# Weights held until the filters' last group, and three small operations moved off VectorE's product chain, in a fused FFT filter and swish MLP kernel

## The chip, the cores and the metric

The kernel runs on one core of one Trainium2 chip. The metric is device time in microseconds (us). A profile of one execution comes with each kernel; its times are also in us, counted from the first instruction. In its lines PE is TensorE's matmuls, PEld its weight loads, DVE is VectorE, ACT is ScalarE, POOL is GpSimd and SPq is the queue in which SyncE issues DMAs. L446 is line 446 of that kernel's source; lines after the change's added line are one higher in the changed kernel.

Runs marked slow are left out: one of the first runs of the kernel before took 1008.37 us. "Rounds" are executions of the kernels compared, taken together; e1 to e7 ran on one chip, e9 to e16 on another, each group with the kernel before beside it. Ratios are the mean time of one kernel's fast runs over that of the other's fast runs of the same rounds, so they are not quite the ratios of the medians that are quoted.

## The reference, cut to what matters

```python
def _attn_ref(x, filt_r, filt_i):          # x: 8 x 3008 x 256
    X = np.fft.rfft(x, axis=1)
    Y = X * (filt_r + 1j * filt_i)[None]   # filters: 1505 x 256
    return np.fft.irfft(Y, n=x.shape[1], axis=1).astype(np.float32)

def _moe_ref(x, w_in, w_out, beta):        # 24064 tokens, 256 -> 2048 -> 256
    h = x @ w_in
    g = h * (1.0 / (1.0 + np.exp(-beta * h)))
    return (g @ w_out).astype(np.float32)
```

The FFT along the sequence is done as matmuls: 3008 = 47 x 64, first a stage over 47, then one over 64 with the filter in between, then both back. `g` is computed as silu(beta * h), and 1/beta is folded into `w_out`.

## The kernel before

Two stretches matter. The **setup** (0 to 38 us) does all of batch 0's FFT. The **main loop** is 752 steps (47 blocks of 512 tokens, 16 feature blocks each): a step is two matmuls `hps`, one SiLU on ScalarE (`gT`) and four matmuls `acc`. Between the steps, the FFT stages of the next batches are woven in.

In the setup, GpSimd waits for a part of the filters (`held`), and only then issues the loads of the weights and of batch 1's input:

```python
# N1 = 47, M = 64, H = 32, NK = 24, KG = 6, J = 32, JG = 8, P = 128
FG = ((0, KG), (KG, KG), (2 * KG, 2 * KG))   # filter groups: first rows and number
# group 0 is issued by GpSimd; groups 1 and 2 by SyncE:
for h in (1, 0):      # group 1: high halves first, then low halves
    ...
for h in (0, 1):      # group 2: low halves first, then high halves
    ...
held = setup.tile([P, 1], F32, name="held", tag="held")
for p0 in (H, M + H):                        # high halves of group 1
    gp.tensor_copy(held[p0 : p0 + H], fri[p0 : p0 + H, 2 * KG - 1, :1])
load_win(0); load_win(1); load_wout(0)       # cut: one per line in the kernel
xs[1] = load_x(1, X_HALVES[:2])              # batch 1, first half
# later, at i == 3: load_wout(1), load_x(1, X_HALVES[2:], xs[1]), load_wout(2), load_wout(3)
```

Twelve pairs of products with the filters then run on VectorE. Around them stand the table copies and beta:

```python
for i in range(NK // 2 + FLAG):
    if 0 < i < NK // 2:
        product(i)           # two VectorE tensor_tensor, pb_t and qb_t, out of PSUM
    ...
    if i in TAB:             # (1, 2, 5, 6, 8, 9): turn a table on PE, copy it from PSUM
        n = TAB.index(i)
        table3(1 + n // 2, 2 - 2 * (n % 2), n % 2 == 0)()   # True: ScalarE copies
    if i == 3:
        ...
        mark3 = dpool.tile([1, D], BF16, name="mark3", tag="mark3")
        nc.sync.dma_start(mark3[:], xs[1][:1, J - 1, :])    # the "marker"
        ...
        nc.tensor.transpose(bps[:], bt[:], id_f[:])
        nc.vector.tensor_copy(beta_sb[:], bps[:])
        nc.vector.reciprocal(rbeta_sb[:], beta_sb[:])
    if i == 9:
        table4()
    if i >= FLAG:
        inverse3(i - FLAG)
...
for at in (0, M):                            # first third of the repeated filters
    for go in load_filter(frr, filt_r, at, 0, JG, nc.sync):
        go()                                 # four loads, 256 KB each, on SyncE
```

Of the kernel before, what the change touches and what calls it, by code (L numbers as in the profile page):

```python
# [11 lines left out]
ACT = mybir.ActivationFunctionType  # L12
# [12 lines left out]
M = 64  # L25
H = M // 2
NK = 24
J = 32
KG = 6
# [8 lines left out]
def kernel(  # L38
# [10 lines left out]
    nc = tc.nc  # L49
# [37 lines left out]
    fri = consts.tile([P, NK, D], F32, name="fri", tag="fri")  # L87
# [10 lines left out]
    beta_sb = consts.tile([P, NFB], F32, name="beta_sb", tag="beta_sb")  # L98
# [6 lines left out]
    def evac(dst, src, on_act, scale=None):  # L105
        if on_act:
            nc.scalar.activation(dst, src, ACT.Copy, scale=1.0 if scale is None else scale)  # L107
        elif scale is None:
            nc.vector.tensor_copy(dst, src)  # L109
        else:  # L110
            nc.vector.tensor_scalar_mul(dst, src, scale)  # L111

    def load_x(b, parts, t=None):
        if t is None:
            t = xpool.tile([NP, J, D], BF16, name="xg", tag="xg")
        xv = x[b].rearrange("(p j) d -> p j d", j=J)
        for p0, p1, j0, j1 in parts:
            nc.gpsimd.dma_start(t[p0:p1, j0:j1, :], xv[p0:p1, j0:j1, :])  # L118
        return t
# [20 lines left out]
    def staged(i):  # L140
        return frr[:, NK - NFB + i * WG : NK - NFB + (i + 1) * WG, :]

    def load_wout(i):
        nc.gpsimd.dma_start(
            staged(i),
            moe_w_out[i * WG * P : (i + 1) * WG * P, :].rearrange("(fb fp) j -> fp fb j", fp=P),
        )
# [52 lines left out]
    gp = nc.gpsimd  # L200
# [75 lines left out]
    def t2_part(h, part):  # L276
        u, r = us[h], rs[h]
        ks_ = slice(h * NH, (h + 1) * NH)
        if part == 0:
            nc.scalar.activation(t2[:, ks_, 2, :], u[:], ACT.Sin, scale=TWO_PI)  # L280
        elif part == 1:
            nc.scalar.activation(r[:], u[:], ACT.Abs)
        else:
            for cols, sgn, b in ((slice(0, H), -1.0, hp), (slice(H, M), 1.0, hm)):
                nc.scalar.activation(
                    t2[:, ks_, 1, cols], r[:, :, cols], ACT.Sin, scale=sgn * TWO_PI, bias=b[:]
                )

    def t2_more(h, eng):
        ks_ = slice(h * NH, (h + 1) * NH)  # L290
        nc.vector.tensor_scalar_mul(t2[:, ks_, 4, :], t2[:, ks_, 1, :], -1.0)
        eng.tensor_copy(t2[:, ks_, 3, :], t2[:, ks_, 2, :])
        eng.tensor_copy(t2[:, ks_, 0, :], t2[:, ks_, 1, :])
# [56 lines left out]
    def table3(i, part, on_act, own=None):  # L350
        pt = own or opsum.tile([P, KG, P], BF16, name="pt", tag="acc")
        for e in range(KG):
            nc.tensor.transpose(
                pt[:, e, :],
                t2[:, KG * i + e, part : part + 2, :].rearrange("p c k -> p (c k)"),
                ident[:],
            )
        dst = t3 if part else t3b

        def go():  # L360
            if i > 0:
                evac(dst[:, KG * i : KG * i + KG, :], pt[:], on_act)
                return
            if part:
                evac(dst[:, 0, :], pt[:, 0, :], on_act, 0.5)
            else:
                nc.vector.tensor_scalar_mul(dst[:, 0, :], pt[:, 0, :], keep[:])
            evac(dst[:, 1:KG, :], pt[:, 1:KG, :], on_act)

        return go  # L370
# [21 lines left out]
    def turn_a(i, on_act):  # L392
        if i % 2 == 0:
            a2s.append(a2pool.tile([P, KG, D], BF16, name="a2", tag="a2"))
        pb = opsum.tile([P, 3, D], BF16, name="pb", tag="acc")
        for e in range(3):
            k1 = 3 * i + e
            for dc in range(NDC):
                nc.tensor.transpose(
                    pb[:, e, dc * P : (dc + 1) * P],  # L400
                    a_t[:, dc, k1, :, :].rearrange("p j a -> p (j a)"),
                    ident[:],
                )
        evac(a2s[-1][:, 3 * (i % 2) : 3 * (i % 2) + 3, :], pb[:], on_act)


    held = setup.tile([P, 1], F32, name="held", tag="held")
    for p0 in (H, M + H):
        gp.tensor_copy(held[p0 : p0 + H], fri[p0 : p0 + H, 2 * KG - 1, :1])
    def load_win(h):  # L410
        fs = slice(h * FF // 2, (h + 1) * FF // 2)
        gp.dma_start(win_sb[:, :, fs], moe_w_in[:, fs].rearrange("(dc p) f -> p dc f", p=P))
# [13 lines left out]
    def product(i):  # L426
        g, kk = divmod(2 * i, KG)
        p_t = pqpool.tile([P, 2, D], BF16, name="pb_t", tag="p_t")
        q_t = pqpool.tile([P, 2, D], BF16, name="qb_t", tag="q_t")
        pss = []  # L430
        for part in (3, 1):
            if part == 3:
                ps = fpsum.tile([P, 2, D], F32, name="ps2", tag="f")
            else:
                ps = hpsum.tile([P, 2, D], F32, name="ps2q", tag="hps")
            for e in range(2):
                nc.tensor.matmul(
                    ps[:, e, :],
                    lhsT=t2[:, 2 * i + e, part : part + 2, :].rearrange("p c k -> p (c k)"),
                    rhs=a2s[g][:, kk + e, :],  # L440
                    start=True,
                    stop=True,
                )
            pss.append(ps)
        for dst, ps in zip((p_t, q_t), pss):
            nc.vector.tensor_tensor(dst[:], ps[:], fri[:, 2 * i : 2 * i + 2, :], ALU.mult)  # L446
        pq[i] = (p_t, q_t)
# [34 lines left out]
    def table4():  # L482
        for src, dst in ((t1b, t4b), (t1, t4)):
            tp = opsum.tile([KP, NP], BF16, name="tp", tag="acc")
            nc.tensor.transpose(tp[:], src[:], ident[:NP, :NP])
            nc.scalar.activation(dst[:], tp[:], ACT.Copy)
# [4 lines left out]
    for i in range(NK // 2 + FLAG):  # L491
        if 0 < i < NK // 2:
            product(i)
        if i % 3 < 2 and i // 3 < 3:
            turn_a(2 + 2 * (i // 3) + i % 3, True)
        if i < 3:
            t2_part(1, i)
        if i in TAB:
            n = TAB.index(i)
            table3(1 + n // 2, 2 - 2 * (n % 2), n % 2 == 0)()  # L500
        if i == 3:
            t2_more(1, nc.vector)
            load_wout(1)
            if B > 1:
                load_x(1, X_HALVES[2:], xs[1])
                mark3 = dpool.tile([1, D], BF16, name="mark3", tag="mark3")
                nc.sync.dma_start(mark3[:], xs[1][:1, J - 1, :])
            load_wout(2)
            load_wout(3)

            bps = hpsum.tile([P, NFB], F32, name="bps", tag="hps")
            nc.tensor.transpose(bps[:], bt[:], id_f[:])
            nc.vector.tensor_copy(beta_sb[:], bps[:])
            nc.vector.reciprocal(rbeta_sb[:], beta_sb[:])
        if i == 9:
            table4()
        if i >= FLAG:
            inverse3(i - FLAG)

# [292 lines left out]
    for s in range(len(steps) + LAG):  # L812
        if s < len(steps):
            i, fb = steps[s]
# [26 lines left out]
        if s >= LAG:  # L841
            i, fb = steps[s - LAG]
# [64 lines left out]
```

## Time and profile before

| | |
|---|---|
| time, first three runs | 792.77 and 792.15 us, and a slow one of 1008.37 |
| profiled run | span 788.4 us |
| PE busy | 777.5 us, 99% |
| first SiLU of the main loop | 38.90 us |

The page's first lines and its chain of waits (shares of the span):

```profile
span 788.4 us, 15540 instructions
PE 777.5 (99%) x6111; PEld 547.9 (69%) x6111; DVE 394.4 (50%) x647; ACT 597.4 (76%) x920; POOL 144.6 (18%) x143
PE 90%; DMA 5%; DVE 3%; issue 1%; POOL 0%; DVEq 0%; ACT 0%; POOLq 0%; SPq 0%; ACTq 0%
```

PE sets the time from the loop's start to its end. A change in the setup can gain only by starting the loop earlier. The timeline of VectorE (start, duration, engine, line, operation, out<-in, shape; in brackets the idle time before) around product 6 and around the last t3b copy:

```profile
25.69 0.68 DVE L446 TENSOR_TENSOR qb_t<-ps2q,fri 128x512 bf16<-128x512 f32 x1
27.01 0.69 DVE L446 TENSOR_TENSOR pb_t<-ps,fri 128x512 bf16<-128x512 f32 x1 [0.64 <-PE ps L437]
27.62 0.68 DVE L446 TENSOR_TENSOR qb_t<-ps2q,fri 128x512 bf16<-128x512 f32 x1
...
31.67 0.68 DVE L446 TENSOR_TENSOR qb_t<-ps2q,fri 128x512 bf16<-128x512 f32 x1
32.27 0.54 DVE L109 COPY t3b<-pt 128x768 bf16<-128x768 bf16 x1
32.73 0.68 DVE L446 TENSOR_TENSOR pb_t<-ps,fri 128x512 bf16<-128x512 f32 x1
```

After product 6 VectorE has no gap until the last product, so whatever ends its wait there sets the loop's start. The bracket names PE, but PE's matmuls for product 6 were over by 25.7 us. This is the case of a wait for several semaphores of which the profile names the wrong one. The trace's raw rows have a semaphore wait of VectorE from 24.23 to 26.87 us, on the semaphores of filter group 2. It really waited for a DMA. And the t3b copy costs 0.46 us of the chain (32.27 to 32.73).

### The profile page before, as it was taken

What the parts mean: (1) busy time and instruction counts of PE and PEld (TensorE: products, weight loads), DVE (VectorE), ACT (ScalarE), POOL (GpSimd) and SP (SyncE); (2) the same over time, 40 slices, a digit from 0 to 9 for tenths busy, and PEclk for the clock granted to TensorE, in tenths of its full rate; (3) what the DMA queues carried; (4) which work ended last, traced back from release to release, by engine and by line L of the source; (5) the groups of instructions that cost most, each with busy time, mean ns of one, the idle gap of its engine ahead of it and who ended that gap; (6) DMA issues with size and microseconds to landing.
All of it is one profiled execution on the core that took longest, in us unless ns stands there. A gap on an engine that the chain in (4) does not pass through costs nothing.

```text
span 788.4 us, 15540 instructions
## 1 busy us (share of the span) xinstructions
PE 777.5 (99%) x6111; PEld 547.9 (69%) x6111; DVE 394.4 (50%) x647; ACT 597.4 (76%) x920; POOL 144.6 (18%) x143
## 2 busy tenths in 40 slices
PE   8899999999999999999999999999999999999997
PEld 5766667766777667876668766686667766776665
DVE  7847835646536564465635746267462761500101
ACT  6887886886678866788677876778767788677776
POOL 9422500420014200131002310024000340000000
PEclk9999999999999999999999999999999999999999
DMA  9978687116901187012860238412370214100101
GB/s 193 233 199 214 161 207 206 48 67 187 234 27 67 48 214 206 28 67 94 198 176 27 95 103 186 151 55 85 103 215 29 74 67 127 51 31 28 54 27 54
DMA packets 84057, 91.46 MB, mean 116 GB/s; under 512 B 4434, under 2 KB 74212, under 8 KB 82962
## 3 DMA queue, kind: packets, MB, share of 16 engines
q1 hardware_dynamic: 80880, 73.95, 30.6%
q0 software_dynamic: 2816, 16.26, 10.6%
q8 instruction: 48, 0.79, 0.4%
q10 hardware_dynamic: 288, 0.26, 0.1%
q14 instruction: 25, 0.20, 0.1%
HBM read 57.16 MB, written 46.66 MB: 132 GB/s over the span
## 4 chain that ended last, share of the span: by engine, by line
PE 90%; DMA 5%; DVE 3%; issue 1%; POOL 0%; DVEq 0%; ACT 0%; POOLq 0%; SPq 0%; ACTq 0%
PE acc L860 40%; PE hps L825 39%; PE ps L621 3%; PE ps L546 2%; PE ps L643 2%; PE ps L669 2%; DMA fri<-in_filt_i_dram 1%; DMA d<-a 1%; DVE ost L109 1%; DMA xg<-in_x_dram 1%; DMA mark<-xg 1%; DMA a<-d 0%; DVE qb_t L446 0%; DVE q_t L658 0%; DVE pb_t L446 0%
## 5 line engine op out<-in xcount | busy, mean ns | idle before, releaser
L834 ACT ACTIVATE gT<-hps,beta_sb 128x512 bf16<-128x512 f32 x752 | 516.8, 687 | 175.2 <-PE hps L825 165.5
L860 PE MATMUL acc<-wout_sb,gT 128*128 128x256 bf16 x3008 | 455.1, 272 | 1.2 <-ACT ost L107 0.2
L825 PE MATMUL hps<-y,win_sb 128*128 128x512 bf16 (+8 forms) x1730 | 447.7, 351 | 0.0
L860 PEld LDWEIGHTS <-gT 128*128 128x128 bf16 x3008 | 285.4, 98 | 132.4 <-issue 4.3
L825 PEld LDWEIGHTS <-win_sb 128*128 128x128 bf16 x1730 | 164.9, 98 | 24.3 <-issue 0.2
L659 POOL TENSOR_TENSOR v_t<-p_t,q_t 128x512 bf16<-128x512 f32 x84 | 106.7, 1271 | 374.5 <-DVE q_t L658 371.6
L109 DVE COPY ost<-acc 128x512 f32<-128x512 f32 (+1 forms) x88 | 56.2, 677 | 193.6 <-PE acc L860 190.6
L109 DVE CAST a<-ps 96x512 bf16<-96x512 f32 x96 | 65.8, 686 | 86.1 <-PE ps L621 83.7
L111 DVE TENSOR_SCALAR y<-ps 128x376 bf16<-128x376 f32 (+1 forms) x119 | 64.4, 545 | 63.1 <-PE ps L546 62.9
L654 DVE TENSOR_TENSOR p_t<-ps,frr 128x512 f32<-128x512 f32 x84 | 58.1, 692 | 32.4 <-PE ps L643 29.8
L658 DVE TENSOR_TENSOR q_t<-ps,fri 64x512 f32<-64x512 f32 x84 | 58.3, 694 | 1.2
L655 DVE SCALAR_TENSOR_TENSOR q_t<-ps,fri 64x512 f32<-64x512 f32 x84 | 57.5, 684 | 1.1
L546 PEld LDWEIGHTS <-zz 96*128 96x128 bf16 x512 | 35.3, 97 | 28.9
L107 ACT ACTIVATE z<-ps 128x512 bf16<-128x512 f32 x84 | 49.5, 590 | 0.8 <-PE ps L669 0.7
L621 PE MATMUL ps<-xg,t 94*96 94x512 bf16 x112 | 41.9, 381 | 0.0
L546 PE MATMUL ps<-t,zz 96*128 96x94 bf16 x448 | 36.7, 204 | 0.0
L118 POOL DMA_DIRECT2D xg<-in_x_dram x22 | 12.1, 557 | 114.3 <-PE acc L860 97.7
L669 PE MATMUL ps<-v_t,t 128*128 128x256 bf16 x168 | 32.1, 273 | 0.6 <-DVE q_t L658 0.6
L643 PE MATMUL ps<-a,t 128*128 128x256 bf16 x168 | 32.1, 273 | 0.3 <-DMA a<-d 0.3
L643 PEld LDWEIGHTS <-t 128*128 128x128 bf16 x168 | 15.9, 98 | 15.0 <-issue 0.4
L621 PEld LDWEIGHTS <-t 94*96 94x96 bf16 x112 | 13.8, 123 | 12.1
L669 PEld LDWEIGHTS <-t 128*128 128x128 bf16 x168 | 15.4, 98 | 8.4 <-DVE q_t L658 1.4
(119 smaller groups left out, 195.8 us busy)
## 6 DMA issues: line engine op xcount, KB each, us to landing
out_dram<-ost SPq DMA_DIRECT2D x80, 256.0 KB, 2.1
d<-a SPq DMA_DIRECT2D x28, 384.0 KB, 3.7
a<-d SPq DMA_DIRECT2D x28, 384.0 KB, 5.1
d<-z SPq DMA_DIRECT2D x28, 384.0 KB, 2.3
zz<-d SPq DMA_DIRECT2D x28, 384.0 KB, 6.6
xg<-in_x_dram POOLq DMA_DIRECT2D x6, 1280.0 KB, 10.1
frr<-in_filt_r_dram SPq DMA_DIRECT2D x12, 256.0 KB, 7.5
out_dram<-ost SPq DMA_DIRECT2D x18, 128.0 KB, 3.6
```

What stands on the lines that cost most here:

```text
L109: nc.vector.tensor_copy(dst, src)
L111: nc.vector.tensor_scalar_mul(dst, src, scale)
L546: nc.tensor.matmul(ps[:, e, :NP], lhsT=zz[:, jj + e, dc * P : (dc + 1) * P], rhs=tab[:], start=True, stop=True,)
L621: nc.tensor.matmul(ps[:KP], lhsT=t1[:], rhs=s["x"][:, 2 * i : 2 * i + 2, :], start=True, stop=True)
L643: nc.tensor.matmul(ps[:, e, :], lhsT=t2[:, k0 + e, 3:5, :].rearrange("p c k -> p (c k)"), rhs=s["a2"][g][:, kk + e, :], start=True, stop=True,
L654: nc.vector.tensor_tensor(p_t[:], ps[:], frr[:, ks_, :], ALU.mult)
L658: nc.vector.tensor_tensor(q_t[:M], ps[M:P], fri[M:P, ks_, :], ALU.mult)
L659: nc.gpsimd.tensor_tensor(v_t[:], p_t[:], q_t[:], ALU.add)
L669: nc.tensor.matmul(ps[:, e, :], lhsT=t3[:, k0 + e, :], rhs=v_t[:, e, :], start=True, stop=True)
L825: nc.tensor.matmul(hps[:, pos - t0 : pos - t0 + ln], lhsT=win_sb[:, dc, fb * P : (fb + 1) * P], rhs=ys[b][:, dc, n0 : n0 + ln], start=(dc ...
L834: nc.scalar.activation(gT[:, :tn], hps[:, :tn], ACT.Silu, scale=beta_sb[:, fb : fb + 1])
L860: nc.tensor.matmul(acc[tb // per][:, tb % per, :], lhsT=gT[:, tb * P : (tb + 1) * P], rhs=wout_sb[:, fb, :], start=(fb == 0 and tb % per = ...
```

## The change

The intent is to give the DMA engines to the filters alone until the last group is (nearly) there, and to take from VectorE what isn't a product while the products run.

```diff
-    for p0 in (H, M + H):
-        gp.tensor_copy(held[p0 : p0 + H], fri[p0 : p0 + H, 2 * KG - 1, :1])
+    for p0 in (0, M):
+        gp.tensor_copy(held[p0 : p0 + H], fri[p0 : p0 + H, NK - 1, :1])
@@ the loop over the products
-            table3(1 + n // 2, 2 - 2 * (n % 2), n % 2 == 0)()
+            table3(1 + n // 2, 2 - 2 * (n % 2), n % 2 == 0 or n == 5)()
@@
+        if i == 11:
+            table4()
 
             bps = hpsum.tile([P, NFB], F32, name="bps", tag="hps")
             nc.tensor.transpose(bps[:], bt[:], id_f[:])
-            nc.vector.tensor_copy(beta_sb[:], bps[:])
+            nc.scalar.activation(beta_sb[:], bps[:], ACT.Copy)
+        if i == NK // 2:
             nc.vector.reciprocal(rbeta_sb[:], beta_sb[:])
-        if i == 9:
-            table4()
```

The gate moves from the high halves of group 1 to the low halves of group 2. (Group 2's high halves, the very last, aren't waited for.) Below, "the gate" is the first part and "the relief" the rest. Beta's transpose and table4 move to the end of the products.

## The prediction

> **What bounds the kernel.** On the profile page TensorE matmuls are busy 777.5 of 788.4 us (99%), and the chain of waits is 90% PE. Everything that the change touches lies in the first 38 us: the first step of the main loop (matmul hps) starts at 38.26 us. From about 17 to 35 us the chain runs through VectorE: the timeline shows 12 pairs of filter products (pb_t, qb_t), 0.68 us each and one every 0.60 us, with few gaps. After 38 us PE is close to saturated, so the change can only shift the loop's start; nothing in the loop itself changes.
>
> **What changes.**
> 1. VectorE loses beta's copy and reciprocal before product 4 (timeline: 23.59 to 23.95, 0.36 us) and the last t3b copy (32.27 to 32.73, 0.46 us). ScalarE takes the t3b copy (its 128x768 copies take 0.81 us, issue about 0.7 us apart) and beta's copy. For that one the Trainium skill, "ScalarE: Activation LUTs", What ACT_TABLE_LOAD costs, gives 186 ns + 0.833 ns per element, so an estimate of 0.2 us; the similarly small t4b copy took 0.24 here. ScalarE is busy 3.08 us of the 5 from 30 to 35 us (windows view), so this fits. The reciprocal (0.25 us) falls into VectorE's 0.36 us hole before z_t. Beta's transpose no longer takes an hps buffer before product 4, for which PE waited 0.37 us at 22.57; late, it holds inverse 9 back until qb_t 10 is done, but inverses 9 and 10 (0.44 us each) fit behind product 11.
> 2. The gate (held) moves from the high halves of filter group 1 to the low halves of group 2. The semaphore landings of those are at about 21.3 and 22.7 us, so GpSimd's weight issue moves from 18.72 to about 23.1 us. Weight packets, however, first moved at about 23.3 us: they stood behind the filters' packets. The Trainium skill, "DMA: Bandwidth & Descriptors", Queues, rings and completion order, says that each engine round-robins between queues; here it looks nearly first come, first served, with mixing only at the tail. So the weights really move by only 0.5 to 1.5 us.
> 3. VectorE's product 6 waited for the last filter transfer: a semaphore wait from 24.23 to 26.87 us, released when its last two DMA engines landed (26.44, 26.83; the other 14 had by 25.4), of which 0.64 us was idle. In those two engines the last ten packets mixed with weights. With weights issued at 23.1 and moving from about 24.3, part of the mixing stays, since the gate is the low half and the high halves land last. I expect landing at about 26.3.
>
> **Sum.** 0.46 us is sure (t3b). The 0.36 us of beta and the 0.64 us of waiting are worth what the landing gains: at most 1.0, expected 0.4. Total 0.9 us, at most 1.5, on the loop's start. Later weights cost nothing: win lands about 28 to 31 (needed 38.3), wout's quarters are scaled four or more us before use, x's first half of batch 1 lands at 36 (needed 39.1). scale_wout(0) moves from 33.0 to about 34.2, needed 40.7.
>
> Predicted: 791.9 us, range 790.4 to 793.4; faster by over 2%: 0.01, within 2%: 0.97, slower: 0.02.
>
> **What would show it.** First hps matmul at about 37.4 instead of 38.26; no t3b copy on VectorE at 32; product pairs 9, 10, 11 without a gap; win's issue at about 23.1; weights landing up to 1.5 us later; the idle before product 6 smaller or gone; nothing different after 45 us but the shift.
>
> **What would make it wrong.** Weights or batch 1's x landing so late that PE waits in the first block; beta's late transpose stalling PE at the products' end; the loop absorbing the shift; run-to-run noise (792.15 to 792.77) larger than the effect, or slow runs such as the one of 1008.

## More of the kernel before

The marker makes SyncE wait until batch 1's second half has landed (it reads a row of the load that brings 80 of its 94 partitions; in the profile before that load landed at 41.08 us and the marker was issued at 41.10). Everything that SyncE issues later stands behind it, in program order: first the four `frr` loads, then the four stores of batch 1's first stage:

```python
apool = pool("apool", 3)                     # three buffers for a1
def s1(b, i, on_act):
    g, jj = divmod(2 * i, JG)
    if jj == 0:
        s["a1"] = apool.tile([KP, JG, D], BF16, name="a1", tag="a1")
    ...                                      # one matmul, ps1
    evac(s["a1"][:, jj : jj + 2, :], ps[:KP], on_act)
    if jj + 2 == JG:
        nc.sync.dma_start(s["d1r"][:, g * JG : (g + 1) * JG, :], s["a1"][:])
```

Batch 1 needs four a1 tiles and there are three buffers, one of them used by batch 0's `zz` at first. So the fourth tile takes the buffer of the first, and may be written only when the first store has landed.

SyncE's queue (its last line here is the first a1 store), and then VectorE's first a1 copy after its wait for that store:

```profile
41.10 0.24 SPq L507 DMA_DIRECT2D mark<-xg  x1
41.38 0.32 SPq L131 DMA_DIRECT2D frr<-in_filt_r_dram  x1
...
43.23 0.39 SPq L626 DMA_DIRECT2D d<-a  x1
```

```profile
50.66 1.31 DVE L109 CAST a<-ps 96x512 bf16<-96x512 f32 x2 [2.33 <-DMA d<-a]
```

VectorE waits 2.33 us for the first store. PE doesn't: from 50 to 56 us it is busy for 6.00 of 6.00 us (the windows view; shown with the result). It still had matmuls to do.

## The result

The changed kernel took 793.41 us (median of 6 runs, 792.48 to 795.84), against 792.15 us (median of the five fast runs) for the kernel before on the same chips. The ratio is 1.0027, with a 95% interval from 1.0006 to 1.0047. So it is within 2%, but slower where 0.9 us of gain was forecast, and 0.01 us above the range.

The page after, and the timelines that answer to those above:

```profile
span 791.7 us, 15448 instructions
PE 771.6 (97%) x6015; PEld 547.6 (69%) x6111; DVE 394.1 (50%) x645; ACT 597.4 (75%) x922; POOL 144.5 (18%) x143
PE 90%; DVE 4%; DMA 3%; issue 2%; ACT 1%; DVEq 0%; ACTq 0%; SPq 0%
```

(Some 96 matmul records are missing from this trace, so PE's busy time isn't compared.)

```profile
26.05 0.69 DVE L446 TENSOR_TENSOR pb_t<-ps,fri 128x512 bf16<-128x512 f32 x1 [1.15 <-DMA fri<-in_filt_i_dram]
...
31.90 0.68 DVE L446 TENSOR_TENSOR qb_t<-ps2q,fri 128x512 bf16<-128x512 f32 x1
32.50 0.68 DVE L446 TENSOR_TENSOR pb_t<-ps,fri 128x512 bf16<-128x512 f32 x1
```

The setup did what was hoped. Product 6 starts 0.96 us earlier, there is no t3b copy at 32 us, and the first SiLU comes at 37.48 instead of 38.90: 1.42 us earlier. Then SyncE's queue, and VectorE's a1 copy:

```profile
43.33 0.24 SPq L507 DMA_DIRECT2D mark<-xg  x1
43.61 0.32 SPq L131 DMA_DIRECT2D frr<-in_filt_r_dram  x1
...
45.47 9.68 SPq L627 DMA_DIRECT2D d<-a  x4
```

```profile
52.74 1.28 DVE L109 CAST a<-ps 96x512 bf16<-96x512 f32 x2 [5.67 <-DMA d<-a]
```

Everything on SyncE is 2.2 us later than in the profile before. VectorE waits 5.67 us for the first store, and now PE waits with it. First, three lines of the changed kernel's list of waits from 46 to 56 us (engine, line, what it waited for: us, times, longest; the list of the kernel before has no wait of PE there). Then PE's busy time from 50 to 56 us, of the kernel before and of the changed one:

```profile
DVE a L109 <- DMA d<-a: 5.7, 1, 5.7
PEld L547 <- issue: 2.9, 1, 2.9
PE ps L547 <- DVE a L109: 2.6, 1, 2.6
```

```profile
50.00:56.00 6.00, 6.00 (x48) 4.02 (x46) 1.67 (x3) 5.47 (x11) 0.00 (x0) 1.00 0.49 138
```

```profile
50.00:56.00 6.00, 3.33 (x26) 2.22 (x26) 1.64 (x3) 3.26 (x7) 0.00 (x0) 1.00 0.72 210
```

The second column of these two is the stretch's length, the third PE's busy time; the third number from the end is the clock that TensorE was granted, as a share of full speed. And the chain of waits of the changed kernel runs, in this stretch, through the store alone:

```profile
45.47 7.16 DMA d<-a
...
52.74 0.70 DVE a L109
...
53.48 0.33 PE ps L547 x4
```

A ledger is useful here. The 752 SiLUs are the same in all kernels, so the start of SiLU number n in one profile minus its start in the first profile of before tells where time was lost. In the changed kernel the difference is -1.42 us at step 0 and -1.26 at step 10. (The 0.16 us go at step 3: batch 1's first half landed at 37.87 us, and PE's first matmul with it could start only at 37.91.) It is +1.52 from step 13 to step 83, +3.31 from step 84, and stays there to the end (+3.34). Two places lose: steps 11 to 13 lose 2.77 us, and step 84 loses 1.79. For the first, the lines give the sum: VectorE's copy is 2.08 us later (50.66 to 52.74) and the loop came 1.26 us earlier to the place. The rest, 2.08 + 1.26 - 2.77 = 0.57 us, is the slack that the kernel before had. The same sum with this slack is tried on three other profiles below the table.

### The profile page after: what moved, and what is told of

Same layout as the page of the kernel before. It is cut to its first block, busy times and chain, and to the rows that moved or that the text cites. A ratio compares the mean times of both kernels' runs of the same rounds, so it can differ in the third digit from the quotient of the medians.

```text
span 791.7 us, 15448 instructions
## 1 busy us (share of the span) xinstructions
PE 771.6 (97%) x6015; PEld 547.6 (69%) x6111; DVE 394.1 (50%) x645; ACT 597.4 (75%) x922; POOL 144.5 (18%) x143
## 4 chain that ended last, share of the span: by engine, by line
PE 90%; DVE 4%; DMA 3%; issue 2%; ACT 1%; DVEq 0%; ACTq 0%; SPq 0%
PE acc L861 41%; PE hps L826 37%; PE ps L622 3%; PE ps L547 3%; PE ps L644 2%; DMA d<-a 2%; PE ps L670 2%; DVE ost L109 1%; DMA a<-d 1%; DVE q_t L659 0%; DVE a_t L109 0%; DVE qb_t L446 0%; DVE q_t L656 0%; ACT a L107 0%; PE pw L187 0%
## 5 line engine op out<-in xcount | busy, mean ns | idle before, releaser
L826 PE MATMUL hps<-y,win_sb 128*128 128x512 bf16 (+8 forms) x1636 | 427.4, 350 | 0.1
```

Of the source, the lines that this page charges most:

```text
L826: nc.tensor.matmul(hps[:, pos - t0 : pos - t0 + ln], lhsT=win_sb[:, dc, fb * P : (fb + 1) * P], rhs=ys[b][:, dc, n0 : n0 + ln], start=(dc ...
```

## The experiments

**Theory A.** The gate makes batch 1's input land later, the marker holds SyncE until then, and the first store, behind the marker and 1 MB of `frr` loads, lands too late for the recycling of the a1 buffers. **Theory B** puts the loss on the work moved to ScalarE and VectorE. Later rivals are named with the runs.

The table has the profile of every run. Columns: the start of product 6 (when the filters' last group is there); the first SiLU; when the first a1 store had landed, from the trace's raw semaphore rows; the us lost against the first profile of before at steps 11 to 16, between step 16 and step 83, and at steps 84 to 88; and the measured ratio to before.

| run | product 6 | first SiLU | store landed | 11-16 | 16-83 | 84-88 | ratio (95%) |
|---|---|---|---|---|---|---|---|
| before | 27.01 | 38.90 | 50.5 | 0 | 0 | 0 | 1 |
| after | 26.05 | 37.48 | 52.6 | +2.77 | 0 | +1.79 | 1.0027 (1.0006 to 1.0047) |
| e1_gate_only | 26.08 | 37.97 | 52.6 | +4.02 | 0 | -0.42 | 1.0030 (1.0014 to 1.0047) |
| e2_relief_only | 27.55 | 38.98 | 52.8 | +1.57 | 0 | -0.42 | 1.0006 (0.9991 to 1.0021) |
| e3_after_frr_late | 26.88 | 38.31 | 48.0 | 0 | +3.62 | +0.54 | 1.0019 (1.0001 to 1.0037) |
| e7_relief_frr_late | 27.21 | 38.65 | 46.1 | 0 | +3.27 | +3.28 | 1.0050 (1.0029 to 1.0071) |
| e9_after_frr_mid | 26.23 | 37.66 | 47.0 | 0 | 0 | +0.74 | 0.9968 (0.9944 to 0.9992) |
| e10_after_frr_mid_nomark | 25.96 | 37.39 | 47.3 | 0 | 0 | +1.00 | 0.9974 (0.9950 to 0.9999) |
| e11_before_frr_mid_nomark | 27.39 | 39.28 | 46.9 | 0 | 0 | -0.36 | 0.9990 (0.9966 to 1.0013) |
| e12_relief_frr_mid_nomark | 27.59 | 39.02 | 47.6 | 0 | 0 | -0.42 | 0.9992 (0.9968 to 1.0017) |
| e13_after_again | 26.18 | 37.61 | 52.4 | +3.68 | 0 | +0.74 | 0.9998 (0.9969 to 1.0026) |
| e14_before_again | 28.27 | 40.17 | 51.4 | 0 | 0 | -0.42 | 0.9981 (0.9953 to 1.0010) |
| e15_frr_mid_beta_early | 26.30 | 37.73 | 47.9 | 0 | 0 | +0.81 | 0.9967 (0.9941 to 0.9993) |
| e16_frr_mid_t3b_vector | 25.78 | 37.68 | 47.7 | 0 | 0 | -0.42 | 0.9953 (0.9922 to 0.9984) |

**What the table doesn't show: the clock.** The traces also record the clock that TensorE was granted. In four of these profiles it stood, within the loop, at half of full speed for 3.41 us, from the end of a stall or up to 1.1 us after it: in e1 from 53.46 us, in e13 from 53.50, in e3 from 72.61, and in e7 twice, from 72.33 and from 137.19. From e13, the windows view of that stretch, and matmuls of its chain of waits before and in it:

```profile
53.50:56.90 3.40, 3.40 (x15) 1.82 (x12) 0.62 (x2) 1.74 (x4) 0.00 (x0) 0.50 0.50 140
```

```profile
42.98 0.44 PE acc L861 x4
43.42 0.45 PE hps L826 x2
...
53.90 0.85 PE acc L861 x4
54.75 0.85 PE hps L826 x2
```

PE is busy all the time there, at half the rate. Half of 3.41 us, about 1.7 us, is an estimate of what each such stretch costs. With it, the sum from the lines closes for the three other profiles that stalled at step 11. The lateness of the a1 copy, plus the lead that the loop had at step 10, minus the slack of 0.57 us, gives 1.56 us for e2 (1.57 measured). It gives 2.37 for e1 and 2.01 for e13, and with the 1.7 added 4.1 and 3.7 (4.02 and 3.68 measured). The changed kernel's first profile had no such stretch, though PE stood idle for 2.62 us in it, and for only 2.22 in e1 and 1.85 in e13; what decides it isn't shown here.

The time of the changed kernel thus depends on chance too. Every run lists its mean granted clock: 0.999 or 1.000 in the profiles without such a stretch, 0.997 or 0.998 in those with one, 0.994 with two. The six runs of e1 have 0.995 to 0.998; the six first runs of the changed kernel 0.996 to 0.999; e9's six 0.999 to 1.000.

### The gate alone

The kernel before with only the first hunk of the diff:

```diff
-    for p0 in (H, M + H):
-        gp.tensor_copy(held[p0 : p0 + H], fri[p0 : p0 + H, 2 * KG - 1, :1])
+    for p0 in (0, M):
+        gp.tensor_copy(held[p0 : p0 + H], fri[p0 : p0 + H, NK - 1, :1])
```

> The kernel before with only the gate moved (weights wait for the low halves of filter group 2); VectorE and ScalarE as before. Theory A (the gate makes batch 1's input land 2 us later, SyncE stands in order behind its marker, so the first stage's stores come late and the recycling of the a1 buffers stalls PE at step 11): first SiLU (gT) about 0.6 us earlier than before's 38.90, because the filters land earlier; the first store of a lands at about 52.6 us as in the changed kernel, and from step 13 on the loop is 1.3 to 1.7 us behind before, whatever the start gained. Time 793 to 795 us, ratio 1.001 to 1.004. Theory B (the loss comes from the moved work on ScalarE and VectorE): ratio 0.999 to 1.000 and no stall at step 11.

Measured: 793.4 us (median of 6), ratio 1.003. The first SiLU is 0.93 us early (0.6 was expected), the store lands at 52.6, and steps 11 to 16 lose 4.02 us. The net delay after step 13 was then 3.1 us, twice the 1.3 to 1.7 expected, so the stall's size was missed and its place was right: about 1.7 us of it is the half clock, which the expectation didn't count. With VectorE's and ScalarE's work as before, the gate alone brings the stall and a loss like that of the change; theory B falls.

### The relief alone

The changed kernel with the old gate:

```diff
-    for p0 in (0, M):
-        gp.tensor_copy(held[p0 : p0 + H], fri[p0 : p0 + H, NK - 1, :1])
+    for p0 in (H, M + H):
+        gp.tensor_copy(held[p0 : p0 + H], fri[p0 : p0 + H, 2 * KG - 1, :1])
```

> The changed kernel with the old gate. Theory A: the last filter transfer lands as before (about 26.8 us), so only the t3b copy's 0.46 us is gained: first SiLU 0.4 to 0.6 us earlier, no stall at step 11 (the first store of a lands at about 50.5 us), loop 0.4 to 0.6 us ahead to the end; ratio 0.9985 to 1.000. Theory B: step 11 or the stage before it is late, ratio above 1.001.

Measured: 791.57 us, ratio 1.0006, not to be told from 1. In its profile the filters landed half a microsecond later than in the first profile of before, and so the first SiLU came no earlier. The expectation of no stall at step 11 was wrong for this execution. The marker was released at 43.50 us, since one of batch 1's DMA shares came late, and 1.57 us was lost. So the old gate doesn't exclude this stall; in the kernel before it was near. It also shows what the marker does while the `frr` loads are in front: in the six profiles with this order, with either gate, the first store landed 8.7 to 9.4 us after the marker was issued (before 41.10 and 50.5, e2 43.50 and 52.8).

### The repeated filters moved out of the way, too far

The changed kernel (e3), and with the old gate (e7), with the first four `frr` loads behind the reads of the second stage:

```diff
-    for at in (0, M):
-        for go in load_filter(frr, filt_r, at, 0, JG, nc.sync):
-            go()
@@ uf(), issued after a2_read(1)
-            for k0 in range(JG, NK, JG)
+            for k0 in range(0, NK, JG)
```

> The changed kernel with the first four loads of the repeated filters (frr) moved on SyncE from before the stores of a to behind the second-stage reads. Theory A: the first store no longer queues behind 1 MB of filters; it is issued at about 43.6 us and lands by 48 instead of 52.6, no wait of VectorE for it and no PE stall at step 11; loop about 1.4 us ahead of before until step 80. Ratio 0.997 to 0.999, unless the later stall at step 84 (1.8 us in the changed kernel's profile) stays; with it 0.999 to 1.001. Rival (the stall is set by the late input alone): the stall at step 11 stays over 1.5 us and the ratio is 1.001 to 1.004.

> Old gate, relieved VectorE, and the frr loads moved behind the second-stage reads as in e3. Theory A: start 0.4 to 0.6 us earlier than before, VectorE's 2.3 us wait for the first store gone, ratio 0.998 to 1.000; e3 is better by up to 1 us since it has the filters' earlier landing too. Rival: the gate costs by contention alone, then this one beats e3 by over 1 us.

Measured: e3 792.82 us, ratio 1.0019; e7 794.24 us, ratio 1.0050. The stall at step 11 is gone in both, as theory A has it. But the loads now come late for their own use, at step 30. VectorE's line in e3:

```profile
69.35 0.69 DVE L651 TENSOR_TENSOR p_t<-ps,frr 128x512 f32<-128x512 f32 x1 [5.02 <-DMA frr<-in_filt_r_dram]
```

The time didn't improve, so the expected times of both were wrong, for a cost that I hadn't counted. In both profiles about 1.7 us of the loss between steps 16 and 83 is the half clock after that wait. Still, the place of the loads decides which wait there is.

### The repeated filters after the second store

The changed kernel with the four loads between the second and the third store (e9):

```diff
@@ s1(), after the store of a1
         if jj + 2 == JG:
             nc.sync.dma_start(s["d1r"][:, g * JG : (g + 1) * JG, :], s["a1"][:])
+            if b == 1 and g == 1:
+                for at in (0, M):
+                    for go in load_filter(frr, filt_r, at, 0, JG, nc.sync):
+                        go()
@@ after the loop over the products
-    for at in (0, M):
-        for go in load_filter(frr, filt_r, at, 0, JG, nc.sync):
-            go()
```

> The changed kernel; the first four frr loads are issued by SyncE after the second store of a instead of before the first one; the marker stays. e3 showed that without them in front there is no stall at step 11, and that behind the second-stage reads they are late themselves (4 us at steps 30 to 32). Here both should be gone: first store issued at 43.5 to 44.2, landed by 48.5; frr landed by about 52, used from 66; start 0.6 to 1.4 us ahead of before's profile and no stall over 0.5 us at steps 11 to 13 and 30 to 32. Ratio 0.997 to 1.000 if the order on SyncE was the whole loss; the rival (the later input and weights cost PE time by themselves) says 1.001 to 1.003.

Measured: 788.68 us (788.2 to 790.98), ratio 0.9968, interval 0.9944 to 0.9992. No stall at steps 11 to 13 nor at 30 to 32. SyncE's queue and the windows view of e9:

```profile
42.62 0.24 SPq L507 DMA_DIRECT2D mark<-xg  x1
42.97 2.21 SPq L623 DMA_DIRECT2D d<-a  x2
45.23 0.53 SPq L131 DMA_DIRECT2D frr<-in_filt_r_dram  x1
```

```profile
50.00:56.00 6.00, 6.00 (x54) 4.32 (x52) 1.42 (x3) 5.59 (x10) 0.00 (x0) 1.00 0.82 201
```

Issue to landing of the first store falls from 7.2 us in the changed kernel to 4.0 here (the view of the store's DMAs; 7.3 in the first profile of before). Of the gain of the start, 1.24 us in this profile, 1.02 us are kept from step 3 to step 83. (The rest goes where PE waits for batch 1's first half.) This version is faster than before in the same rounds. Its slowest run, 790.98 us, is also below the changed kernel's fastest of all its runs, 791.58, but that comparison is across different rounds.

### With and without the marker, and on the other kernels

The marker's two lines are taken out as well, for the changed kernel (e10), the kernel before (e11) and the relief alone (e12):

```diff
-                mark3 = dpool.tile([1, D], BF16, name="mark3", tag="mark3")
-                nc.sync.dma_start(mark3[:], xs[1][:1, J - 1, :])
```

> As e9, also without the marker copy that holds SyncE until batch 1's input has landed. The first store is issued when its data are there (about 41.8 us). If the marker was what made the store late, it lands 1 to 2 us earlier than in e9; if the weights ahead in the DMA rings are what it waits for, it lands when it did in e9 (47 to 48.5 us). Time as e9 within 1 us either way, ratio 0.997 to 1.000.

> The kernel before with the same two edits as e10. If the kernel before often loses a part at step 11 too (its profile is one of its fastest runs and shows 2.3 us of VectorE's wait for the first store hidden in slack), ratio 0.997 to 0.9995; if it does not, 0.9995 to 1.001.

> e10 with the old gate. Theory: the gate's own worth is the earlier landing of the last filter group, 0.5 to 1 us, so e10 is better than this one by that much; t3b's 0.46 us makes this one better than e11. Ratio 0.9975 to 1.000. Rival: the gate is worth nothing or less even with the order on SyncE mended; then this one is level with e10 or better.

Measured: e10 789.6 us, ratio 0.9974; e11 790.93, 0.9990; e12 791.29, 0.9992. In e10 the first store is issued at 41.67 us, 1.3 us before e9's, and lands at 47.3, e9's at 47.0. So once the `frr` loads are out of the way, the marker's wait isn't what makes the store late. The store then waits for what the DMA engines were given before it. In e10's trace SyncE's queue (q1) moved no packet until 44.82 us, 3.1 us after the store was issued; from 42 to 44 us all packets were of GpSimd's queue (q0), which carries batch 1's input and the weights:

```profile
DMA packets 159, 0.58 MB, mean 291 GB/s; under 512 B 18, under 2 KB 18, under 8 KB 158
q0 software_dynamic: 159, 0.58, 100.2%
```

In the changed kernel the `frr` loads stood ahead of it too. Two other remedies weren't tried, and would have told more: the marker taken out with the `frr` loads left in front, and a fourth a1 buffer. With the order on SyncE mended, the gate pays: product 6 is at 25.96 us in e10 and at 27.59 in e12, and e10's median is 1.7 us below e12's. The intervals overlap, so for the times this is an indication; for the starts the profiles show it. e11 is level with before, so before isn't shown to lose at step 11 often.

### Again, and the relief in two parts

> The changed kernel once more, for a second profile. If the step-11 stall belongs to the change, steps 11 to 13 lose 2 to 3 us again and the first store lands at 52 to 53 us; the filters land before 26.3 us again. The step-84 loss (1.8 us in the first profile) returns only if it belongs to the change; if it is chance (one late DMA engine of a second-stage read), it is anything from -0.5 to 2.5.

> The kernel before once more, for a second profile: the first one was one of its fastest runs. Expected: filters land at 26.8 to 27.4 us; a stall of 0 to 1.5 us at steps 11 to 13 depending on when one slow DMA engine finishes batch 1's input (41 to 43.5 us); ratio 0.999 to 1.001 by construction.

The changed kernel and the kernel before, unedited, had a second profile (e13, e14). The changed kernel stalls again at steps 11 to 13 (3.68 us; VectorE waits 4.91 us for the store), and the kernel before again doesn't. But in these later rounds the times were 792.33 us for both, ratio 0.9998 (0.9969 to 1.0026). The kernel before against itself gave 0.9981 (0.9953 to 1.0010). So the loss of the change, 0.27% in the first rounds and 0.30% with the gate alone, is of the size by which groups of rounds differ, and is not clear of it. The stall repeats in both profiles of the changed kernel and in e1; its net is about 0 to 2 us. The gain of e9 is of that size too, but four variants with the loads behind the second store and the new gate (e9, e10, e15, e16) all have intervals below 1 (e9 and e10 share the runs of before, and so do e15 and e16).

e15 is e9 with beta's copy and reciprocal back on VectorE before product 4; e16 is e9 with the last t3b copy back on VectorE:

```diff
@@ e15: at i == 3, instead of at i == 11 and i == NK // 2
+            bps = hpsum.tile([P, NFB], F32, name="bps", tag="hps")
+            nc.tensor.transpose(bps[:], bt[:], id_f[:])
+            nc.vector.tensor_copy(beta_sb[:], bps[:])
+            nc.vector.reciprocal(rbeta_sb[:], beta_sb[:])
@@ e16
-            table3(1 + n // 2, 2 - 2 * (n % 2), n % 2 == 0 or n == 5)()
+            table3(1 + n // 2, 2 - 2 * (n % 2), n % 2 == 0)()
```

> e9 with beta's copy and reciprocal back on VectorE before product 4. Theory: they cost nothing there, as VectorE waits over 1 us for the filters before product 6 anyway: first SiLU as e9's (37.66) within 0.25 us after allowing for the filters' landing; time as e9 within 1 us. Rival: 0.36 us later.

> e9 with the last turned table copied by VectorE as before. Theory: it stands behind product 9 on the chain, so first SiLU 0.46 us later than e9's for the same landing of the filters; time 0.2 to 0.8 us above e9's, hardly clear of noise.

Measured: e15 790.07 us, first SiLU 0.06 us after e9's, as product 6 is. Beta's move is worth nothing at the start. e16: 788.93 us, the best ratio of all, 0.9953. Its first SiLU comes 11.90 us after product 6, and e9's 11.43 us. This difference is in the whole table: 11.89 or 11.90 us in the five profiles with t3b on VectorE, 11.43 in the nine with t3b on ScalarE. So t3b's copy costs 0.46 us of the start, exactly as read from the timeline. That e16 is nevertheless not slower than e9 comes from step 84, where e9 lost 0.74 us and e16 nothing.

**What stays open: step 84.** There the second stage of batch 2 starts, with reads that SyncE issues once the last a store of batch 2 has landed. In the profiles that lost nothing there (-0.42), the read was issued 10.0 to 10.4 us after that store was; in those that lost 0.5 us or more, 10.6 to 11.1 (e11, with -0.36, lies between at 10.55). In the changed kernel one of the first read's 16 shares landed at 135.6 us, 2 us after the others. Losses came in the profiles with both the new gate and t3b on ScalarE (six of six, 0.54 to 1.79) and in e7 (3.28, of which about 1.7 is the half clock). I have no cause for that, and the 1.79 us of the first profile after is partly chance: the same kernel lost 0.74 in e13.

## Why the prediction was right or wrong

- **What bounds the kernel, and where the change can act:** right. The loop only shifts, except where PE waits.
- **t3b's copy, 0.46 us "sure":** right. 11.90 against 11.43 us from product 6 to the first SiLU, in fourteen profiles. ScalarE took it without harm at the start: its copy took 0.81 us at 29.80 us, as predicted.
- **Beta's copy, reciprocal and late transpose:** the forecast that the 0.36 us counts only as far as the filters land earlier was right; VectorE still waited 1.15 us before product 6, so it was worth nothing (e15). The 16-element copy took 0.18 us; the estimate from the Trainium skill's "ScalarE: Activation LUTs", What ACT_TABLE_LOAD costs, was 0.2. PE did wait 0.73 us at the late transpose, and as predicted that cost nothing.
- **The gate's move to 23.1 us, and a weight shift of 0.5 to 1.5 us:** the issue came at 23.42. The weights themselves landed 1.6 us later (the first half of `win` at 29.8 instead of 28.2), but batch 1's second half landed 2.2 us later (43.31 instead of 41.08). Not all of that is the gate's: over the profiles its mean is 42.3 us with the old gate (six, 41.1 to 43.6) and 43.3 with the new (eight, 42.6 to 43.8), so the gate's part is about 1 us. In the first pair of profiles the rest is chance. Here the size was missed.
- **The filters' landing:** expected at about 26.3 us, that is 0.4 us gained; 0.96 us was gained in the profile (product 6 at 26.05 instead of 27.01). Over the profiles the mean of product 6 is 27.50 us with the old gate (six) and 26.18 with the new (eight), 1.3 us. The mechanism was right and the size too small: the start gained 1.42 us, where 0.9 was expected and 1.5 called the most.
- **The step that failed:** "Later weights cost nothing". It checked `win`, `wout` and the first half of batch 1's input against their uses. It didn't check the second half, which no compute needed early, but on which a marker on SyncE waited, with four `frr` loads and the first a1 store behind it, and with the a1 buffers behind that store. The slack there was 0.57 us. The start's own gain took more than that (1.26), and the later landing took 2.08 more, so that steps 11 to 13 lost 2.77 us and the loop was 1.52 us behind where a lead of 0.9 was forecast. (The check of the first half was too loose as well: it was needed at 39.1 us before, but at about 37.7 with the earlier start, and landed at 37.87. That cost 0.16 us, and 0.53 in e13.) "Weights or batch 1's x landing so late that PE waits in the first block" was on the list of what would make it wrong; it should have been worked out.
- **"Nothing different after 45 us but the shift":** wrong, at steps 11 to 13, and at step 84. The prediction also didn't count that the clock can fall to half after a stall, as it did in e1 and e13.

## What to carry to other kernels

When a stage is made to start earlier, look at the next place where it meets something timed by DMA: the gain is kept only as far as there is slack, and an earlier start eats the slack as surely as a later transfer. When transfers are held back, follow each issuing queue in program order behind the held transfer, through to the buffers that its stores free. Here the held transfer's own consumer had time enough; what stood behind it in the queue had not. And a wait can cost more than its length: after some of these stalls the matmuls ran at half clock for 3.41 us more. Moving four loads behind two stores turned a loss of 0 to 2 us into a gain of about 2 to 3 (1.7 to 3.4 by the medians of e9, e10, e15 and e16 against before in their rounds).

## What the Trainium skill lacked or had wrong

- "DMA: Bandwidth & Descriptors", Queues, rings and completion order: the page says that each engine round-robins between the queues that it has work for. Here weights issued on GpSimd's queue at 18.72 us moved no packet until 23.38 us (the raw DMA rows), while SyncE's earlier filters drained. From 19 to 23 us all 581 packets were of SyncE's queue:

```profile
DMA packets 581, 0.84 MB, mean 210 GB/s; under 512 B 37, under 2 KB 556, under 8 KB 556
q1 hardware_dynamic: 581, 0.84, 98.4%
```

  So delaying their issue by 4.7 us (to 23.42) delayed their first packet, and the landing of `win`'s first half, by only 1.6 us. In the changed kernel, with the filters nearly through, the first weight packet moved at 24.94 us, 1.5 us after issue, where the page's Specifications give a first-byte latency of about 1 us for DMAs issued by GpSimd. In e10 it was the other way round: the store on SyncE's queue moved nothing for 3.1 us while GpSimd's queue drained. Why the queues didn't mix isn't shown.
- The same page, Anatomy of one DMA: the fit of 2.0 us plus bytes over 436 kB per us is for DMAs issued by GpSimd; the page has none for SyncE's. Used as a rough estimate for a 384 KB store of SyncE it gives 2.9 us. In this stage the store took 4.0 us (e9) to 7.3 us (before), by what had been issued ahead. The page has no rule for such a backlog; e10 shows that an earlier issue by 1.3 us gains nothing then.
- No page that I read says how much one kernel's time differs between groups of rounds: here the kernel before against itself gave 0.9981 (0.9953 to 1.0010), and medians of 791.16 to 792.33 us.
